# More key heads on VectorE and a 512-wide p V product in a decode attention kernel bound by its cache loads

## The chip, the cores and the metric

One core of one Trainium2 chip runs the whole program. The metric is the time of one execution on the device, in microseconds (us). Most executions of the kernel before agree within 0.3%, but it has a second cluster some 1 to 2 us higher in a few executions.

Five engines share the work: TensorE (PE, with its weight loads as PEld), VectorE (DVE), ScalarE (ACT), GpSimd (POOL) and SyncE (SP), which issues the loads. In the profile L286 is line 286 of the kernel.

## The reference, cut to what matters

```python
q = layernorm(x) @ wq                         # 32 heads of 128
k, v = k_cache[:, :, Sk-4096:], v_cache[:, :, Sk-4096:]
p = softmax(q k^T / sqrt(128))                # one query row per head, 4096 keys
s = (p v) @ wo                                # 512 outputs
out = x + s * silu(B(layernorm(x), w1, w2, w3, w4))
```

Each head reads 1 MB of keys and 1 MB of values in bf16, 64 MB in all; weights make it 79 MB. Nothing is used twice, so the loads are a floor under any schedule.

## The kernel before: the parts that matter

Heads come in groups of four. Every even head is scored on VectorE (a product with the broadcast query, then a sum along the head dimension), every odd one on TensorE: 32 transposes, evicted by ScalarE in four blocks of eight, then 32 matmuls of one column.

```python
if h % 2 == 0:
    nc.vector.tensor_tensor(out=prod, in0=kn, in1=q_bc[...], op=ALU.mult)
    nc.vector.tensor_reduce(out=s["sS"][:, hl // 2, :], in_=prod, axis=AX.X, op=ALU.add)
else:
    for b in range(NB):                       # NB = 4
        pt = ps_tr.tile([P, 8, P], BF16, tag="pt")          # three PSUM banks in turn
        for i in range(8):
            nc.tensor.transpose(pt[:, i, :], kn[:, b * 8 + i, :], ident_bf[:])
        nc.scalar.copy(out=kt[:, b * 8:(b + 1) * 8, :], in_=pt[:])
    ...
if hl == G - 1:
    softmax(g)        # two maxima, all-reduce on GpSimd, two subtractions, exp
```

Values follow four heads later. Each is 32 matmuls with one moving column (the probabilities) against 128x128 of values, summed in PSUM; the four heads of a group are scaled by one VectorE instruction. After a block of heads its outputs are repacked (`repack`) and multiplied with wo (`apply_wo`).

```python
for c in range(NC):                           # NC = 32
    nc.tensor.matmul(oT[:, k:k + 1], lhsT=v[:, c, :], rhs=s["pT"][..., c:c + 1],
                     start=(c == 0), stop=(c == NC - 1))
```

## Time and profile before

| | before |
|---|---|
| time, median of 3 | 198.69 us (198.66 to 200.05) |
| profiled span | 196.8 us |
| VectorE / TensorE / ScalarE busy | 126.9 / 119.4 / 69.3 us |
| mean granted TensorE clock | 0.667 |
| loads, from 30 to 187 us | about 424 GB/s, no gap |

How to read it: no engine is above 64% busy, and the chain that ended last is made of 71% loads. The lines are in the prediction. Two more are the busy share of the DMA engines in 40 slices (9 is 90% or more), and the granted clock in tenths.

```profile
PEclk9999999695585555576766667555555585575555
DMA  6999899999999999999999999999999999999960
```

The loads fill every slice to the end, and TensorE is at half clock for most of the second part.

### The profile page before, as it was taken

The numbers are of one execution on the slowest core, as the hardware profiler recorded it, in microseconds if no ns is written. First come the engines' busy times: TensorE is split into PE (matmuls) and PEld (weight loads), VectorE is DVE, ScalarE is ACT, GpSimd is POOL, SyncE is SP. The second block draws the span as 40 slices with busy tenths as digits, with TensorE's granted clock in tenths as the row PEclk, the third lists the DMA queues.
The fourth block names the chain that finished last, engine by engine and source line by source line (L and its number), as shares of the span: only waits on it lengthen the run. The fifth ranks groups of instructions, "written<-read, shape, count | busy, mean of one in ns | idle before, by whom it ended". The sixth has DMA issues, their size and how long they took to land.

```text
span 196.8 us, 5237 instructions
## 1 busy us (share of the span) xinstructions
PE 119.4 (61%) x2399; PEld 108.4 (55%) x2399; DVE 126.9 (64%) x140; ACT 69.3 (35%) x82; POOL 4.9 (3%) x17
## 2 busy tenths in 40 slices
PE   0315896851969474684829293756665654929443
PEld 0314745841969473583829292656565653929332
DVE  1225049998959993959387937959198929594301
ACT  2000329742565243070707070242525250707000
POOL 1011000000000000000000000000000000000000
PEclk9999999695585555576766667555555585575555
DMA  6999899999999999999999999999999999999960
GB/s 185 383 485 446 355 416 421 426 426 421 426 421 423 421 421 425 423 425 420 426 421 428 421 425 416 425 420 426 423 428 423 425 418 425 421 426 422 426 268 10
DMA packets 11349, 79.17 MB, mean 402 GB/s; under 512 B 1376, under 2 KB 1984, under 8 KB 2368
## 3 DMA queue, kind: packets, MB, share of 16 engines
q1 hardware_dynamic: 11176, 78.85, 96.3%
q8 instruction: 18, 0.29, 0.6%
q10 hardware_dynamic: 152, 0.00, 0.0%
q14 instruction: 3, 0.02, 0.0%
HBM read 78.84 MB, written 0.00 MB: 401 GB/s over the span
## 4 chain that ended last, share of the span: by engine, by line
DMA 71%; DVE 12%; issue 6%; PE 6%; ACT 2%; POOL 1%; SPq 0%; POOLq 0%
DMA kv<-in_A_v_cache_dram 40%; DMA kv<-in_A_k_cache_dram 30%; DVE sS L265 7%; DVE prod L262 3%; ACT kt L272 1%; PE a_ps L202 1%; PE qT_ps L221 1%; PE oT L364 1%; PE qb_ps L230 1%; PE h_ps L135 1%; PE y_ps L135 0%; PE ln_ps L140 0%; PE ln_ps L152 0%; ACT q_bc L232 0%; POOL ln_rstd_x L158 0%
## 5 line engine op out<-in xcount | busy, mean ns | idle before, releaser
L272 ACT COPY kt<-pt 128x1024 bf16<-128x1024 bf16 x64 | 60.2, 1025 | 73.0 <-PE pt L271 73.0
L265 DVE TENSOR_REDUCE sS<-prod 128x32 f32<-128x4096 bf16 x16 | 70.7, 4419 | 0.5
L271 PE MATMUL pt<-ident_bf,kv 128*128 128x128 bf16 x512 | 53.8, 298 | 18.2 <-DMA kv<-in_A_k_cache_dram 17.7
L271 PEld LDWEIGHTS <-kv 128*128 128x128 bf16 x512 | 49.8, 140 | 19.7 <-DMA kv<-in_A_k_cache_dram 18.7
L364 PEld LDWEIGHTS <-kv 128*128 128x128 bf16 x1024 | 30.0, 102 | 30.5 <-DMA kv<-in_A_v_cache_dram 22.8
L262 DVE TENSOR_TENSOR prod<-kv,q_bc 128x4096 bf16<-128x4096 bf16 x16 | 36.5, 2283 | 11.0 <-DMA kv<-in_A_k_cache_dram 8.8
L364 PE MATMUL oT<-pT,kv 128*128 128x1 bf16 x1024 | 32.6, 165 | 17.6 <-DMA kv<-in_A_v_cache_dram 17.3
L243 PE MATMUL sT<-qT_bf,kt 128*128 128x1 bf16 x512 | 20.4, 166 | 2.6 <-ACT kt L272 2.3
L243 PEld LDWEIGHTS <-kt 128*128 128x128 bf16 x512 | 18.3, 103 | 3.4 <-ACT kt L272 3.2
L300 PE MATMUL den_ps<-pT,ones_bf 128*128 128x128 bf16 x8 | 2.0, 253 | 16.9 <-ACT pT L294 16.9
L371 DVE TENSOR_TENSOR o<-oT,rden 128x4 bf16<-128x4 f32 x7 | 1.1, 162 | 17.3 <-PE oT L364 17.3
L294 ACT ACTIVATE pT<-e 128x128 bf16<-128x128 f32 x8 | 2.5, 309 | 16.5 <-DVE e L290 16.5
L140 PEld LDWEIGHTS ln_ps<-x_f,ones_f 128*128 128x128 f32 x4 | 1.0, 312 | 11.3 <-DVE x_f L182 6.4
L287 POOL PARTITION_ALL_REDUCE mb<-m x8 | 3.0, 373 | 162.5 <-DVE m L285 162.5
L205 ACT ACTIVATE a_bf<-a_ps 128x10 bf16<-128x10 f32 x1 | 0.2, 180 | 17.4 <-PE a_ps L202 17.4
L302 DVE TENSOR_REDUCE den<-den_ps 128x4 f32<-128x128 f32 x8 | 2.3, 292 | 5.5 <-PE den_ps L300 5.5
L135 PEld LDWEIGHTS <-ox 128*1 128x1 bf16 x112 | 2.5, 113 | 5.3 <-DVE ox L341 5.3
L367 DVE TENSOR_TENSOR o<-oT,rden 128x1 bf16<-128x1 f32 x4 | 0.6, 161 | 7.2 <-PE oT L364 7.2
L230 PE MATMUL qb_ps<-wq_sb,xn_rep 128*128 128x512 bf16 x16 | 5.2, 497 | 0.0
L135 PE MATMUL y_ps<-wo,ox 128*1 128x128 bf16 x112 | 3.7, 306 | 2.3 <-DVE ox L341 2.3
L140 PE MATMUL ln_ps<-x_f,ones_f 128*128 128x4 f32 x4 | 1.2, 365 | 5.9 <-DVE x_f L163 4.9
L290 DVE TENSOR_TENSOR e<-sS,mb 128x64 f32<-128x64 f32 x8 | 1.8, 224 | 3.9 <-POOL mb L287 3.9
(79 smaller groups left out, 48.2 us busy)
## 6 DMA issues: line engine op xcount, KB each, us to landing
kv<-in_A_k_cache_dram SPq DMA_DIRECT2D x32, 1024.0 KB, 19.7
kv<-in_A_v_cache_dram SPq DMA_DIRECT2D x32, 1024.0 KB, 19.7
wq_sb<-in_A_wq_dram SPq DMA_DIRECT2D x1, 4096.0 KB, 19.2
wo<-in_A_wo_dram SPq DMA_DIRECT2D x3, 1024.0 KB, 20.4
w_sb<-in_B_w_dram SPq DMA_DIRECT2D x1, 1376.0 KB, 7.9
w_sb<-in_B_w_dram SPq DMA_DIRECT2D x1, 1024.0 KB, 10.2
w_sb<-in_B_w_dram SPq DMA_DIRECT2D x1, 512.0 KB, 3.7
wo<-in_A_wo_dram SPq DMA_DIRECT2D x1, 512.0 KB, 19.8
```

Source lines behind the costliest of these rows:

```text
L135: nc.tensor.matmul(ps[32 * j:32 * j + 1, :], lhsT=col, rhs=w[0:k, j * P:(j + 1) * P], start=False, stop=last, skip_group_check=True)
L140: nc.tensor.matmul(ps[:], lhsT=ones_f[:], rhs=src_f, start=True, stop=True)
L230: nc.tensor.matmul(qb_ps[:], lhsT=xn_rep[:, c, :], rhs=wq_h[:, c, 2 * i:2 * i + 8:2, :], start=(c == 0), stop=(c == KC - 1))
L243: nc.tensor.matmul(sT[:, hl // 2, c:c + 1], lhsT=kt[:, c, :], rhs=qT_bf[:, h:h + 1], start=True, stop=True)
L262: nc.vector.tensor_tensor(out=prod[:], in0=kn[:], in1=q_bc[:, h // 2:h // 2 + 1, :].to_broadcast([P, NC, Dh]), op=ALU.mult)
L265: nc.vector.tensor_reduce(out=s["sS"][:, hl // 2, :], in_=prod[:], axis=AX.X, op=ALU.add)
L271: nc.tensor.transpose(pt[:, i, :], kn[:, b * 8 + i, :], ident_bf[:])
L272: nc.scalar.copy(out=kt[:, b * 8:(b + 1) * 8, :], in_=pt[:])
L287: nc.gpsimd.partition_all_reduce(mb[:], m1[:], channels=P, reduce_op=ReduceOp.max)
L294: nc.scalar.activation(out=pT[:], in_=e[:], func=ACT.Exp, scale=scale)
L302: nc.vector.tensor_reduce(out=den[:], in_=den_ps[:], axis=AX.X, op=ALU.add)
L364: nc.tensor.matmul(oT[:, k:k + 1], lhsT=v[:, c, :], rhs=s["pT"][:, hl % 2, hl // 2, c:c + 1], start=(c == 0), stop=(c == NC - 1))
```

## The change

The intent: use VectorE, which looks a third idle, for 20 heads instead of 16, so that TensorE and ScalarE have 12 heads to transpose instead of 16; and make the value product cheaper in instructions, eight matmuls with 512 moving columns of values instead of 32 with one. The eight matmuls leave, for each head, four rows of four blocks of 128 sums, of which only the block with the row's own number is wanted; four small fp32 matmuls with a selection matrix (`add`) pick and add these for a whole group. The last group keeps the narrow form. The PSUM bank of the new accumulator is taken from the transposes, which have two banks now, not three. Four tiny loads of x, which nothing reads, are issued behind the seventh key head (`i == 6`) among the loads.

```diff
-    ps_tr = ctx.enter_context(tc.tile_pool(name="ps_tr", bufs=3, space=PSUM))
+    ps_tr = ctx.enter_context(tc.tile_pool(name="ps_tr", bufs=2, space=PSUM))
+    ps_v = ctx.enter_context(tc.tile_pool(name="ps_v", bufs=1, space=PSUM))
     ... 
+    def places(g):                            # heads of a group: on VectorE, on TensorE
+        if g % 2 == 0:
+            return slice(0, 3, 1), slice(3, 4, 1)
+        return slice(0, 4, 2), slice(1, 4, 2)
     ... (queries, softmax and denominators in this order)
-        for c in range(NC):
-            nc.tensor.matmul(oT[:, k:k + 1], lhsT=v[:, c, :], rhs=s["pT"][:, hl % 2, hl // 2, c:c + 1], ...)
+            for c in range(0, NC, 4):
+                nc.tensor.matmul(s["ov"][32 * hl:32 * hl + 4], lhsT=s["pT"][:, hl, c:c + 4],
+                                 rhs=v[:, c:c + 4, :], start=False, stop=c == NC - 4, ...)
+            if hl == G - 1:
+                nc.scalar.copy(out=s["ov_sb"][:], in_=s["ov"][:])
     ...
+            def add(s=s, o=o, at=h - h0 - 3):
+                oT = ps_o.tile([P, G], FP32, tag="oT", name="oT")      # one buffer
+                for j in range(4):
+                    nc.tensor.matmul(oT[:], lhsT=s["ov_sb"][:, j, :], rhs=pick_f[:, j, :], ...)
+                nc.vector.tensor_tensor(out=o[:, at:at + G], in0=oT[:], in1=s["rden"][:], op=ALU.mult)
     ...
+        if i == 6:
+            for n in (1, 2, 4, 8):
+                mk = small.tile([n, D // n], BF16, name=f"mk{n}")
+                load(mk[:], A_x.rearrange("a b (p n) -> (a b p) n", p=n))
```

So even groups now have three heads on VectorE and one on TensorE, odd groups two and two.

More of the change, by code (lines that the diff above doesn't have):

```diff
@@ L214, with on_vector @@
     nc.scalar.activation(out=g_row[:], in_=bv[:], func=ACT.Silu)
-    qT_ps = ps_misc.tile([P, H], FP32, tag="misc", name="qT_ps")
-    for h in range(1, H, 2):
+    def places(g):
+        if g % 2 == 0:
+            return slice(0, 3, 1), slice(3, 4, 1)
+        return slice(0, 4, 2), slice(1, 4, 2)
+    def on_vector(h):
+        s_pl = places(h // G)[0]
+        return h % G in range(G)[s_pl]
+    pe_heads = [h for h in range(H) if not on_vector(h)]
+    ve_heads = [h for h in range(H) if h % 2 == 0] + list(range(1, H, 2 * G))
+    assert sorted(pe_heads + ve_heads) == list(range(H))
+    q_at = {h: i for i, h in enumerate(ve_heads)}
+    q_at.update({h: i for i, h in enumerate(pe_heads)})
+    qT_ps = ps_misc.tile([P, len(pe_heads)], FP32, tag="misc", name="qT_ps")
+    for i, h in enumerate(pe_heads):
         for c in range(KC):
-            nc.tensor.matmul(qT_ps[:, h:h + 1], lhsT=wq_sb[:, c, h * Dh:(h + 1) * Dh],
+            nc.tensor.matmul(qT_ps[:, i:i + 1], lhsT=wq_sb[:, c, h * Dh:(h + 1) * Dh],
                              rhs=xn_bf[:, c:c + 1], start=(c == 0), stop=(c == KC - 1))
-    qT_bf = small.tile([P, H], BF16, name="qT_bf")
-    nc.vector.tensor_copy(out=qT_bf[:, 1::2], in_=qT_ps[:, 1::2])
-    q_bc = small.tile([P, H // 2, Dh], BF16, name="q_bc")
+    qT_bf = small.tile([P, len(pe_heads)], BF16, name="qT_bf")
+    nc.vector.tensor_copy(out=qT_bf[:], in_=qT_ps[:])
+    q_bc = small.tile([P, len(ve_heads), Dh], BF16, name="q_bc")
     wq_h = wq_sb[:].rearrange("p c (h d) -> p c h d", d=Dh)
-    for i in range(0, H // 2, 4):
+    for i in range(0, len(ve_heads), 4):
         qb_ps = ps_tr.tile([P, 4, Dh], FP32, tag="pt", name="qb_ps")
+        h0, step = ve_heads[i], ve_heads[i + 1] - ve_heads[i]
         for c in range(KC):
-            nc.tensor.matmul(qb_ps[:], lhsT=xn_rep[:, c, :], rhs=wq_h[:, c, 2 * i:2 * i + 8:2, :],
+            nc.tensor.matmul(qb_ps[:], lhsT=xn_rep[:, c, :], rhs=wq_h[:, c, h0:h0 + 3 * step + 1:step, :],
                              start=(c == 0), stop=(c == KC - 1))
@@ L239, with qk @@
     rows_open(y_ps)
-    def qk(sT, hl, h, kt):
+    def qk(sT, i, h, kt):
         for c in range(NC):
-            nc.tensor.matmul(sT[:, hl // 2, c:c + 1], lhsT=kt[:, c, :], rhs=qT_bf[:, h:h + 1],
+            nc.tensor.matmul(sT[:, i, c:c + 1], lhsT=kt[:, c, :],
+                             rhs=qT_bf[:, q_at[h]:q_at[h] + 1],
                              start=True, stop=True)
+    pick_f = const.tile([P, 4, G], FP32, name="pick_f")
+    nc.vector.tensor_copy(out=pick_f[:], in_=ident_bf[:].rearrange("p (h i) -> p i h", h=G)[:, 0:4, :])
     pending = []
@@ L256, in k_head @@
                 "sT": ps_s.tile([P, G // 2, NC], FP32, tag="sT", name="sT"),
-                "sS": sm_pool.tile([P, G // 2, NC], FP32, tag="sS", name="sS"),
+                "sS": sm_pool.tile([P, G - 1, NC], FP32, tag="sS", name="sS"),
             }
         s = st[g]
-        if h % 2 == 0:
+        on_v, on_t = places(g)
+        if on_vector(h):
             prod = prod_pool.tile([P, NC, Dh], BF16, tag="prod", name="prod")
             nc.vector.tensor_tensor(out=prod[:], in0=kn[:],
-                                    in1=q_bc[:, h // 2:h // 2 + 1, :].to_broadcast([P, NC, Dh]),
+                                    in1=q_bc[:, q_at[h]:q_at[h] + 1, :].to_broadcast([P, NC, Dh]),
                                     op=ALU.mult)
-            nc.vector.tensor_reduce(out=s["sS"][:, hl // 2, :], in_=prod[:], axis=AX.X, op=ALU.add)
+            nc.vector.tensor_reduce(out=s["sS"][:, range(G)[on_v].index(hl), :], in_=prod[:], axis=AX.X, op=ALU.add)
         else:
@@ L274, in k_head @@
                     flush()
-            pending.append((s["sT"], hl, h, kt))
+            pending.append((s["sT"], range(G)[on_t].index(hl), h, kt))
             if hl == G - 1:
@@ L282, in softmax @@
         s = st[g]
-        m1 = sm_pool.tile([P, 2, G // 2], FP32, tag="m1", name="m1")
-        nc.vector.tensor_reduce(out=m1[:, 0, :], in_=s["sS"][:], axis=AX.X, op=ALU.max)
-        nc.vector.tensor_reduce(out=m1[:, 1, :], in_=s["sT"][:], axis=AX.X, op=ALU.max)
-        mb = sm_pool.tile([P, 2, G // 2], FP32, tag="mb", name="mb")
+        parts = []
+        for pl, src in zip(places(g), (s["sS"], s["sT"])):
+            n = len(range(G)[pl])
+            parts.append((pl, n, src[:, 0:n, :]))
+        m1 = sm_pool.tile([P, G], FP32, tag="m1", name="m1")
+        for pl, n, src in parts:
+            nc.vector.tensor_reduce(out=m1[:, pl], in_=src, axis=AX.X, op=ALU.max)
+        mb = sm_pool.tile([P, G], FP32, tag="mb", name="mb")
         nc.gpsimd.partition_all_reduce(mb[:], m1[:], channels=P, reduce_op=ReduceOp.max)
-        e = sm_pool.tile([P, 2, G // 2, NC], FP32, tag="e", name="e")
-        for i, src in enumerate((s["sS"], s["sT"])):
-            nc.vector.tensor_tensor(out=e[:, i], in0=src[:],
-                                    in1=mb[:, i, :].unsqueeze(2).to_broadcast([P, G // 2, NC]),
+        e = sm_pool.tile([P, G, NC], FP32, tag="e", name="e")
+        for pl, n, src in parts:
+            nc.vector.tensor_tensor(out=e[:, pl, :], in0=src,
+                                    in1=mb[:, pl].unsqueeze(2).to_broadcast([P, n, NC]),
                                     op=ALU.subtract)
-        pT = sm_pool.tile([P, 2, G // 2, NC], BF16, tag="pT", name="pT")
+        pT = sm_pool.tile([P, G, NC], BF16, tag="pT", name="pT")
         nc.scalar.activation(out=pT[:], in_=e[:], func=ACT.Exp, scale=scale)
@@ L357, in v_head @@
             softmax_den(g)
-            s["oT"] = ps_o.tile([P, G], FP32, tag="oT", name="oT")
+            if i == last_block:
+                s["oT"] = ps_o.tile([P, G], FP32, tag="oT", name="oT")
+            else:
+                s["ov"] = ps_v.tile([P, 4, Dh], FP32, tag="ov", name="ov")
+                nc.tensor.matmul(s["ov"][:], lhsT=zero_bf[:], rhs=v[:, 0:4, :], start=True, stop=False,
+                                 skip_group_check=True)
         if h == h0:
             o_blk[i] = sm_pool.tile([P, n], BF16, tag="o", name="o")
-        k = 2 * (hl % 2) + hl // 2
-        oT, o = s["oT"], o_blk[i]
-        for c in range(NC):
-            nc.tensor.matmul(oT[:, k:k + 1], lhsT=v[:, c, :], rhs=s["pT"][:, hl % 2, hl // 2, c:c + 1],
-                             start=(c == 0), stop=(c == NC - 1))
-        if i == last_block:
-            nc.vector.tensor_tensor(out=o[:, h - h0:h - h0 + 1], in0=oT[:, k:k + 1],
-                                    in1=s["rden"][:, k:k + 1], op=ALU.mult)
-        elif hl == G - 1:
-            nc.vector.tensor_tensor(
-                out=o[:, h - h0 - 3:h - h0 + 1].rearrange("p (a b) -> p b a", b=2),
-                in0=oT[:].rearrange("p (b a) -> p b a", b=2),
-                in1=s["rden"][:].rearrange("p (b a) -> p b a", b=2), op=ALU.mult)
+        o = o_blk[i]
+        if i == last_block:
+            oT = s["oT"]
+            for c in range(NC):
+                nc.tensor.matmul(oT[:, hl:hl + 1], lhsT=v[:, c, :], rhs=s["pT"][:, hl, c:c + 1],
+                                 start=(c == 0), stop=(c == NC - 1))
+            nc.vector.tensor_tensor(out=o[:, h - h0:h - h0 + 1], in0=oT[:, hl:hl + 1],
+                                    in1=s["rden"][:, hl:hl + 1], op=ALU.mult)
+        else:
+            for c in range(0, NC, 4):
+                nc.tensor.matmul(s["ov"][32 * hl:32 * hl + 4], lhsT=s["pT"][:, hl, c:c + 4],
+                                 rhs=v[:, c:c + 4, :], start=False, stop=c == NC - 4,
+                                 skip_group_check=True)
+            if hl == G - 1:
+                s["ov_sb"] = sm_pool.tile([P, 4, Dh], FP32, tag="ov_sb", bufs=2, name="ov_sb")
+                nc.scalar.copy(out=s["ov_sb"][:], in_=s["ov"][:])
         ready, later[:] = later[:], []
@@ L377, in v_head @@
             f()
-        if h == h0 + n - 1 and i < last_block:
+        if hl == G - 1 and i < last_block:
+            def add(s=s, o=o, at=h - h0 - 3):
+                oT = ps_o.tile([P, G], FP32, tag="oT", name="oT")
+                for j in range(4):
+                    nc.tensor.matmul(oT[:], lhsT=s["ov_sb"][:, j, :], rhs=pick_f[:, j, :],
+                                     start=(j == 0), stop=(j == 3))
+                nc.vector.tensor_tensor(out=o[:, at:at + G], in0=oT[:], in1=s["rden"][:], op=ALU.mult)
             def step(i=i, n=n):
@@ L381, in step @@
                 later.append(lambda: [apply_wo(i, t) for t in range(n)])
-            later.append(step)
+            later.append(lambda: [add(), later.append(step)] if h == h0 + n - 1 else add())
     v_pool = None
```

## The prediction

> **What bounds the kernel now.** I read the chain that ended last, then the group rows of the page, then VectorE in order of time, then the last microseconds. From the page: busy totals, chain by engine, and the rows of the two instructions of a head on VectorE and of the transpose eviction:
>
> ```profile
> PE 119.4 (61%) x2399; PEld 108.4 (55%) x2399; DVE 126.9 (64%) x140; ACT 69.3 (35%) x82; POOL 4.9 (3%) x17
> ...
> DMA 71%; DVE 12%; issue 6%; PE 6%; ACT 2%; POOL 1%; SPq 0%; POOLq 0%
> ...
> L265 DVE TENSOR_REDUCE sS<-prod 128x32 f32<-128x4096 bf16 x16 | 70.7, 4419 | 0.5
> L262 DVE TENSOR_TENSOR prod<-kv,q_bc 128x4096 bf16<-128x4096 bf16 x16 | 36.5, 2283 | 11.0 <-DMA kv<-in_A_k_cache_dram 8.8
> ```
>
> The transfers set the end: 71% of the chain is key and value loads, and from 30 us to 187 us the DMA engines move about 424 GB/s without a gap. VectorE's product waits 8.8 us for keys. But the share of 64% understates VectorE: its first head starts only at 27.4 us, when the queries are there, so 119.8 of the 158 us from 27 to 185 are busy, 76%. One cycle of it, from VectorE's timeline:
>
> ```profile
> 66.63 2.29 DVE L262 TENSOR_TENSOR prod<-kv,q_bc 128x4096 bf16<-128x4096 bf16 x1
> 68.95 4.42 DVE L265 TENSOR_REDUCE sS<-prod 128x32 f32<-128x4096 bf16 x1
> 73.41 0.22 DVE L284 TENSOR_REDUCE m<-sS 128x2 f32<-128x64 f32 x1
> 75.42 0.16 DVE L371 TENSOR_TENSOR o<-oT,rden 128x4 bf16<-128x4 f32 x1 [1.79 <-PE oT L364]
> 75.62 0.23 DVE L332 TENSOR_TENSOR spread<-o,mt 128x64 bf16<-128x64 bf16 x1
> 75.76 0.21 DVE L285 TENSOR_REDUCE m<-sT 128x2 f32<-128x64 f32 x1
> 76.47 0.23 DVE L290 TENSOR_TENSOR e<-sS,mb 128x64 f32<-128x64 f32 x1 [0.50 <-POOL mb L287]
> 76.61 0.22 DVE L290 TENSOR_TENSOR e<-sT,mb 128x64 f32<-128x64 f32 x1
> 77.52 0.29 DVE L302 TENSOR_REDUCE den<-den_ps 128x4 f32<-128x128 f32 x1 [0.69 <-PE den_ps L300]
> ...
> 78.38 0.27 DVE L341 TENSOR_REDUCE ox<-pick 128x8 bf16<-128x64 f32 x1
> 78.56 2.28 DVE L262 TENSOR_TENSOR prod<-kv,q_bc 128x4096 bf16<-128x4096 bf16 x1
> ```
>
> A head costs 73.41 - 66.63 = 6.78 us. The softmax is a round trip VectorE, GpSimd, VectorE, ScalarE, TensorE, VectorE, and VectorE waits in place (0.50 and 0.69 us), because the next product stands behind it. The end, from the timeline of all engines:
>
> ```profile
> 191.93 1.01 PE L364 MATMUL oT<-pT,kv 128*128 128x1 bf16 x32 [1.45 <-DMA kv<-in_A_v_cache_dram]
> 192.93 0.60 PE L135 MATMUL y_ps<-wo,o 128*1 128x128 bf16 x16
> 192.98 0.16 DVE L367 TENSOR_TENSOR o<-oT,rden 128x1 bf16<-128x1 f32 x1 [2.30 <-PE oT L364]
> 193.58 0.29 DVE L404 TENSOR_TENSOR y<-y_ps,g_row 128x128 f32<-128x128 f32 x1 [0.43 <-PE y_ps L135]
> ```
>
> The last value head's data starts its matmuls at 191.93; the block of heads 24 to 27 had been finished at 186.
>
> **What the Trainium skill says.** "TensorE: Matmul & The Clock Gate", Back-to-back issue gap: a moving operand of N columns costs N / 1.2 ns cold and N / 2.4 + 2.5 ns warm, thus 427 or 216 ns for 512. This trace agrees: the 16 qb_ps matmuls of 512 take 5.19 us, which is 8 at 0.43 and 8 at 0.216, and the clock record turns full in their middle. Part 1 there (clock gate) says a busy window of about 3.4 us must pass before the clock rises; the mean granted clock here is 0.667. "Runtime: NRT & Kernel Launch", Instruction fetch mechanics: instructions are refilled in 16 KiB blocks of 256. The queue table here agrees: 18 instruction packets, 0.29 MB. "DMA: Bandwidth & Descriptors", Why a DMA increments its semaphore by 16 and not by 1: a load of 1, 2, 4 or 8 rows uses only that many engines. No run here shows it yet.
>
> **The change part by part.**
> - VectorE takes 20 heads, not 16: four more at 6.78, +27.1 us. Even groups have three, odd groups two.
> - ScalarE loses 16 evictions of about 1 us and gains 7 of a 128x512 fp32 tile (0.59 us, the q_bc row). It had slack: no gain.
> - TensorE: 28 heads change from 32 one-column matmuls (1.0 us a head) to 8 of 512 columns: 8 x 0.216 = 1.73 us warm, 3.46 cold. Fewer instructions, but more time. Seven groups gain four fp32 matmuls; one fp32 128x4 matmul of the layer norm is two passes, 0.22 us apart and 0.37 long, so four take 7 x 0.22 + 0.37 = 1.9 us.
> - Startup: 4 more qb_ps, 16 fewer qT_ps matmuls: the first product starts 16 x 0.029 = 0.46 us earlier, and the release of the query weights moves about 1 us later, with key loads still in flight until 35 us. No effect.
> - Four tiny loads take four of the eight completion slots that the load queue uses in turn. For about 10 us four big loads are in flight instead of eight, still about 10 us of work. No effect either way.
> - Instructions: TensorE's listed ones fall from 4788 to 2929, so some 7 fewer fetch packets of 16 KB, at 424 GB/s about 0.3 us in the mean; perhaps 1.5 us on the engine that ends last. Counts only if transfers still set the end.
>
> **VectorE's schedule, laid out by hand** in the order of the built program, with e(g) the moment when group g's second subtraction ends:
> - Heads 0, 1, 2 start at 27.0 and end at 47.3; then the maximum, the product of head 4, and e(0) = 50.2. Heads 4 and 6 are through at 62. TensorE does values 0 to 2 (one cold, two warm: 7.0 us from 51), then key head 7 with value 3 (about 6): 64.4. So e(1) is about 65.5, where it was 58.8, and head 8, whose key landed at 55, starts about 12 us late.
> - Odd to even: 1.35 to the next product (softmax remainder), 3 x 6.78 = 20.3, and 1.3 for maxima, reduction and subtractions: 23.0.
> - Even to odd: VectorE alone needs 1.75 + 2 x 6.78 + 0.2 = 15.5. But the maximum of the TensorE heads waits for a chain in TensorE's program order that starts only with this softmax: denominators, repack and 32 output matmuls (76.83 to 79.72 before, 2.9) and the opening matmul (0.3), value a (1.7 to 3.5), keys with value b (5.1 to 8.3, paced by the four 0.94 us evictions), value c (1.7 to 3.5), keys with value d (5.4 to 8.3). Sum 17.1 warm, 27 cold; I take 19.5, the first value cold and the rest mostly warm. Plus 1.07 from the maximum to e: 20.6.
> - The pair is 43.6 us, while the loads bring eight heads in 42.35 (keys 14 and 30 landed at 87.6 and 172.3). So the delay of 12 us is never won back. e(7) = 65.5 + 23.0 + 3 x 20.6 + 2 x 23.0 = 196.3, against 183.7 before.
> - Then 0.7 to the denominators and four value heads of 1.0 us with 0.25 between, as at 185.90 and 187.16: last value product ends at 201.8, not 192.94: +8.9.
>
> Value buffers do not choke this: value 31 needs buffer 24 free at about 182 instead of 172, with 17 us of loads in flight.
>
> **Tail.** The single PSUM buffer of oT is held by the last group, and in the built order the addition of heads 24 to 27 now stands behind the last value matmul. So 0.25 (scaling), 1.9 (four fp32), then scaling to output matmuls 1.1 (0.20 + 0.25 + 0.21 + 0.21 + 0.23), 32 output matmuls 1.0, while before the end came 0.64 after the product: +3.6.
>
> Sum: 198.7 + 8.9 + 3.6 = 211.2.
>
> **Rivals.**
> 1. Transfers still set the end. For it: 64% on VectorE looks idle, and bytes are unchanged. Against: the wait-in-place above. Then only tail and fetches count: 198.7 + 3.6 - 0.3 to 1.5 = 201 to 202.
> 2. VectorE binds, but TensorE stays warm: chain 17.1, three pairs shorter by 2.4 each: 204. This is the side on which I may err most.
> 3. TensorE stays cold: chain 27, three times 7.5 more: 233. Against: the value matmuls stream densely, so they should lift the clock above 0.667.
> 4. A gain: fewer instructions and a higher clock pay off. That needs TensorE or ScalarE on the chain now; together they have 8% of it, and the tail grows anyway.
>
> **Range and chances.** Rival 1 gives the floor, 201; a half-cold TensorE gives 217. I keep my sum a little lower because VectorE's waits may overlap better than I laid out: 210.5, with 202.5 to 217. Slower by over 2% means over 202.7: 0.88. Within 2%: 0.1. Faster: 0.02.
>
> **What would show it.** VectorE near 154 us busy, hardly waiting for key loads after 60 us; the product after softmax 1 near 67 us; waits of 2 to 6 us on TensorE's sT before the maxima of the odd groups; the chain with VectorE and TensorE in front and the value loads nearly gone; DMA digits falling before the end; a granted clock above 0.7; fp32 oT matmuls after the last value product. If VectorE still waits for keys at 130 us and the last value product starts at its landing near 191, rival 1 holds and only the tail is left.

## The result, and the profile after

| same rounds, same chip | before | after |
|---|---|---|
| median of 4 | 199.37 us (198.66 to 200.19) | 211.28 us (209.07 to 211.63) |
| profiled span | 196.8 us | 209.3 us |
| VectorE / TensorE / ScalarE busy | 126.9 / 119.4 / 69.3 us | 153.3 / 129.3 / 59.5 us |
| mean granted clock | 0.667 | 0.821 |
| packets of instructions (q8) | 18 | 12 |

The kernel got slower: ratio 1.0573, 95% interval 1.0482 to 1.0663. A ratio here is the mean time of one kernel's runs over that of the other's of the same rounds, so it is not quite the ratio of the medians quoted.

The prediction counted by e(g), the moment when group g's second subtraction ends; the same mark is used here, read from VectorE's timeline, and a "stretch" is the time from one e to the next. First the page of the kernel after: busy totals, clock, DMA slices, chain by engine, and two group rows (busy, mean ns | idle before, releaser).

```profile
PE 129.3 (62%) x1522; PEld 78.1 (37%) x1522; DVE 153.3 (73%) x149; ACT 59.5 (28%) x74; POOL 6.9 (3%) x17
...
PEclk9999999755699996559999955589999755599955
DMA  6999999999999999999999999999999999996000
...
DVE 45%; PE 35%; issue 8%; ACT 7%; POOL 3%; POOLq 0%; ACTq 0%; DVEq 0%
...
L404 PE MATMUL ov<-kv,pT 128*4 128x512 bf16 x224 | 54.2, 428 | 1.2 <-DMA kv<-in_A_v_cache_dram 1.2
...
L313 DVE TENSOR_REDUCE m<-sT 128x1 f32<-128x32 f32 (+1 forms) x8 | 1.6, 203 | 15.9 <-PE sT L260 15.9
```

The loads are gone from the chain, where they had 71%, and the DMA digits fall three slices before the end: the data is there, the engines are late. VectorE waits 15.9 us for TensorE's scores in front of its maxima. VectorE in order of time, from one even softmax to the next odd one (duration in the second column, the wait and its releaser in brackets):

```profile
90.42 4.42 DVE L289 TENSOR_REDUCE sS<-prod 128x32 f32<-128x4096 bf16 x1
94.87 2.29 DVE L286 TENSOR_TENSOR prod<-kv,q_bc 128x4096 bf16<-128x4096 bf16 x1
97.20 4.42 DVE L289 TENSOR_REDUCE sS<-prod 128x32 f32<-128x4096 bf16 x1
101.65 0.22 DVE L313 TENSOR_REDUCE m<-sS 128x2 f32<-128x64 f32 x1
106.67 0.23 DVE L313 TENSOR_REDUCE m<-sT 128x2 f32<-128x64 f32 x1 [4.80 <-PE sT L260]
...
108.90 2.26 DVE L286 TENSOR_TENSOR prod<-kv,q_bc 128x4096 bf16<-128x4096 bf16 x1
```

VectorE is through with its two heads at 101.62, but the maximum of the TensorE heads comes only at 106.67. No product can start before that softmax is out of VectorE's way. What TensorE does meanwhile, from its own timeline:

```profile
86.77 0.26 PE L328 MATMUL den_ps<-pT,ones_bf 128*128 128x128 bf16 x1 [8.78 <-ACT pT L322]
...
89.73 3.58 PE L404 MATMUL ov<-kv,pT 128*4 128x512 bf16 x8
93.24 1.19 PE L295 MATMUL pt<-ident_bf,kv 128*128 128x128 bf16 x16
95.14 0.61 PE L295 MATMUL pt<-ident_bf,kv 128*128 128x128 bf16 x8 [0.71 <-ACT kt L296]
...
99.03 1.89 PE L404 MATMUL ov<-kv,pT 128*4 128x512 bf16 x8
100.86 1.07 PE L295 MATMUL pt<-ident_bf,kv 128*128 128x128 bf16 x16
...
104.26 1.89 PE L404 MATMUL ov<-kv,pT 128*4 128x512 bf16 x8
106.08 0.55 PE L260 MATMUL sT<-qT_bf,kt 128*128 128x1 bf16 x16
```

TensorE idled 8.78 us before the denominators. Then the four values and two key heads go through it one after the other: the first value cold (eight matmuls in 3.58 us), the later ones warm (1.89), each key pass about 5.8 us from its first transpose to the next value or to the last score (the second value stands inside the first pass, the fourth inside the second).

In the odd-to-even stretches three values stand directly behind one another, and there the trace shows what the text of the change does not: the matmuls of neighbouring heads, which write different rows of the accumulator, start in pairs (4 to 6 ns apart at 154 us), so that 24 of them take 3.62 to 4.10 us instead of 3 x 1.89. In the even-to-odd stretch a key pass stands between the values, and this is lost. A program that keeps the values together there was not tried. The end, from the timeline of all engines:

```profile
201.65 0.16 DVE L400 TENSOR_TENSOR o<-oT,rden 128x1 bf16<-128x1 f32 x1 [1.08 <-PE oT L398]
201.86 1.87 PE L417 MATMUL oT<-pick_f,ov_sb 128*128 128x4 f32 x8 [0.26 <-DVE o L400]
...
204.84 0.60 PE L136 MATMUL y_ps<-wo,ox 128*1 128x128 bf16 x16 [0.48 <-DVE ox L369]
205.22 0.64 PE L136 MATMUL y_ps<-wo,o 128*1 128x128 bf16 x16
205.92 0.29 DVE L451 TENSOR_TENSOR y<-y_ps,g_row 128x128 f32<-128x128 f32 x1 [1.13 <-PE y_ps L136]
```

The scaling of the last value product ends at 201.65 + 0.16 = 201.81 (before, by the prediction's third fence: 192.98 + 0.16 = 193.14); the fp32 addition of heads 24 to 27 and their repacking follow in the open, and the final product starts at 205.92, 4.11 us behind that scaling, where it was 0.44.

### The profile page after: what moved, and what is told of

The parts are those of the page before. It is cut to its first block, busy times and chain, and to the rows that moved or that the text cites. A ratio compares the mean times of both kernels' runs of the same rounds, so it can differ in the third digit from the quotient of the medians.

```text
span 209.3 us, 3495 instructions
## 1 busy us (share of the span) xinstructions
PE 129.3 (62%) x1522; PEld 78.1 (37%) x1522; DVE 153.3 (73%) x149; ACT 59.5 (28%) x74; POOL 6.9 (3%) x17
## 4 chain that ended last, share of the span: by engine, by line
DVE 45%; PE 35%; issue 8%; ACT 7%; POOL 3%; POOLq 0%; ACTq 0%; DVEq 0%
DVE sS L289 25%; PE ov L404 17%; DVE prod L286 13%; ACT kt L296 5%; PE pt L295 5%; PE sT L260 3%; POOL mb L315 2%; PE y_ps L136 2%; PE oT L398 2%; DVE e L318 1%; PE a_ps L203 1%; ACT pT L322 1%; DVE m L313 1%; PE den_ps L328 1%; PE oT L417 1%
## 5 line engine op out<-in xcount | busy, mean ns | idle before, releaser
L289 DVE TENSOR_REDUCE sS<-prod 128x32 f32<-128x4096 bf16 x20 | 88.4, 4419 | 0.6
L296 ACT COPY kt<-pt 128x1024 bf16<-128x1024 bf16 x48 | 45.6, 1022 | 64.9 <-PE pt L295 64.8
L404 PE MATMUL ov<-kv,pT 128*4 128x512 bf16 x224 | 54.2, 428 | 1.2 <-DMA kv<-in_A_v_cache_dram 1.2
L286 DVE TENSOR_TENSOR prod<-kv,q_bc 128x4096 bf16<-128x4096 bf16 x20 | 45.7, 2284 | 2.6 <-ACT q_bc L249 2.2
L295 PE MATMUL pt<-ident_bf,kv 128*128 128x128 bf16 x384 | 29.6, 229 | 14.8 <-ACT kt L296 8.6
L295 PEld LDWEIGHTS <-kv 128*128 128x128 bf16 x384 | 24.5, 103 | 25.0 <-issue 17.6
L404 PEld LDWEIGHTS <-pT 128*4 128x4 bf16 x224 | 16.4, 91 | 33.6 <-issue 17.5
L260 PE MATMUL sT<-qT_bf,kt 128*128 128x1 bf16 x384 | 14.8, 164 | 1.3 <-ACT kt L296 1.3
L313 DVE TENSOR_REDUCE m<-sT 128x1 f32<-128x32 f32 (+1 forms) x8 | 1.6, 203 | 15.9 <-PE sT L260 15.9
L417 PE MATMUL oT<-pick_f,ov_sb 128*128 128x4 f32 x56 | 8.2, 270 | 1.4 <-ACT ov_sb L409 1.1
L417 PEld LDWEIGHTS oT<-pick_f,ov_sb 128*128 128x128 f32 x56 | 7.6, 210 | 2.0 <-ACT ov_sb L409 1.7
## 6 DMA issues: line engine op xcount, KB each, us to landing
wo<-in_A_wo_dram SPq DMA_DIRECT2D x3, 1024.0 KB, 20.6
```

The source lines that it names most:

```text
L260: nc.tensor.matmul(sT[:, i, c:c + 1], lhsT=kt[:, c, :], rhs=qT_bf[:, q_at[h]:q_at[h] + 1], start=True, stop=True)
L286: nc.vector.tensor_tensor(out=prod[:], in0=kn[:], in1=q_bc[:, q_at[h]:q_at[h] + 1, :].to_broadcast([P, NC, Dh]), op=ALU.mult)
L289: nc.vector.tensor_reduce(out=s["sS"][:, range(G)[on_v].index(hl), :], in_=prod[:], axis=AX.X, op=ALU.add)
L404: nc.tensor.matmul(s["ov"][32 * hl:32 * hl + 4], lhsT=s["pT"][:, hl, c:c + 4], rhs=v[:, c:c + 4, :], start=False, stop=c == NC - 4, skip_g ...
L417: nc.tensor.matmul(oT[:], lhsT=s["ov_sb"][:, j, :], rhs=pick_f[:, j, :], start=(j == 0), stop=(j == 3))
```

## The experiments

All twelve give the right result. Each was timed against the kernel before on the same chip in the same rounds; that kernel's median was 198.70 us in the first four runs, 198.73 in the next four, 198.77 in the next three and 198.77 in the last one. "Base" says from which kernel an edit starts. Ratios are to the kernel before of the same rounds; where two variants are compared with each other, as in "below the kernel after", it is by their medians and traces, from different rounds.

### One half of the change at a time

**Heads alone** (base after): 20 and 12 heads, two transpose banks and tiny loads stay, all values in the narrow form (the edit is cut to its main lines).

```diff
+    def wide(g):
+        return False
-            if i == last_block:               # the narrow form
+            if i == last_block or not wide(g):
```

> 20 and 12 heads as in the changed kernel, but every group's values in the old form of 32 one-column matmuls. My theory (20 heads on VectorE fit as long as TensorE's chain behind the even softmax stays under VectorE's 15.5 us): the pair of groups falls under the 42.35 us of the loads, the delay of about 7 us at the start is won back, 198 to 200.5 us. Rival (VectorE's 27 us of extra work are the loss by themselves): 205 us or more.

Measured: 200.08 us (199.95 to 202.21), ratio 1.0074 (1.0018 to 1.0131), as expected. VectorE is 153.1 us busy, as in the kernel after, but does not pay: the stretch from an even softmax to the next odd one takes 17.1 and 17.4 us in the middle, from odd to even 23.0, so 40.0 and 40.4 for a pair of groups. The last value head waits for its data again:

```profile
193.04 1.01 PE L401 MATMUL oT<-pT,kv 128*128 128x1 bf16 x32 [1.27 <-DMA kv<-in_A_v_cache_dram]
```

**Values alone** (base after): 16 and 16 heads again, values 512 wide.

```diff
-        if g % 2 == 0:
-            return slice(0, 3, 1), slice(3, 4, 1)
-    ve_heads = [h for h in range(H) if h % 2 == 0] + list(range(1, H, 2 * G))
+    ve_heads = [h for h in range(H) if h % 2 == 0]
```

> Values in the 512-wide form as in the changed kernel, but heads split 16 and 16 as before. My theory: transfers set the last value's landing again, and only the tail is paid: 198.7 + 3.6 - up to 1.5 for fewer instruction fetches = 200.8 to 202.3. Rival (the slower value product alone delays TensorE's chain): 205 us or more. If both this and the run with the heads alone come out near the kernel before, the loss needs both parts.

Measured: 203.42 us (203.32 to 203.58), ratio 1.0215 (1.0162 to 1.0268), so 1.1 above the expectation. From its list of VectorE's waits (total, times, longest):

```profile
DVE m L311 <- PE sT L258: 26.4, 7, 5.3
```

VectorE waits for TensorE in all seven stretches, 26.4 us, more than in the kernel after, and yet this is not what sets the end: where no load is waited for a stretch is 18.6 to 20.6 us, e(7) comes at 186.3, and the last value again waits for its load (its matmuls start at 193.05). It starts 1.1 us later than before (191.93), which fits the slower packets of the section on the tiny loads, and behind it stands the fp32 tail, 4.1 us from the end of the last value's scaling to the final product.

So each half stays under the 42.35 us in which eight heads are loaded. With heads alone VectorE needs 23.0 us in one stretch of a pair, but the other is 17.1 to 17.4. With values alone TensorE needs up to 20.6 in each, which is 41.2 for two. With both, the one stretch is VectorE's (22.6) and the other TensorE's (21.5 to 21.9), and the pair is 44.0 to 44.6.

### Where the values hurt

**Even groups narrow** (base after; odd groups stay wide):

```diff
+    def wide(g):
+        return g % 2 == 1
```

> The changed kernel, but the value heads of even groups (three key heads on VectorE, one on TensorE) go back to 32 one-column matmuls with VectorE's scaling of four columns; odd groups keep the 512-wide form. My theory: the loss sits in the stretch from an even softmax to the next odd one, where the value heads of the even group and two key heads pass through TensorE one after the other before the maximum of the TensorE heads. With narrow values there that chain falls under VectorE's own 15.5 us, a pair of groups takes about 40.5 us, less than the 42.35 in which eight heads are loaded, the last value head waits for its data again, and heads 24 to 27 leave no fp32 addition behind it: 199.5 to 201.5 us, e(7) near 187. Rival: it is TensorE's total load of 512-wide matmuls, wherever they stand: removing half of it gives about half of the loss back, 204 to 206, and the same in the run with the odd groups narrow.

Measured: 201.99 us (201.40 to 202.12), ratio 1.0142 (1.0099 to 1.0185): 9.3 us of the loss gone, and 0.5 above the range expected. Stretches from even to odd are 18.6, 19.0 and 21.9 us, from odd to even 22.6, 21.6 and 21.6. e(7) comes at 188.65 us, 7.9 earlier than in the kernel after; the other 1.3 are behind it, where the edit also removes the fp32 addition of heads 24 to 27. Loads are in the chain again, though the last four value heads, against the expectation, wait for none:

```profile
DMA 50%; DVE 22%; PE 12%; issue 9%; POOL 2%; ACT 2%; POOLq 0%; ACTq 0%; SPq 0%; DVEq 0%
```

Part of what is left has a name: the odd group's fp32 addition needs the one output buffer that the next group's narrow values hold, so it comes late and VectorE waits 1.96 us for it in front of a maximum, three times.

**Odd groups narrow** (base after; even groups stay wide):

```diff
+    def wide(g):
+        return g % 2 == 0
```

> The mirror image: odd groups narrow, even groups 512-wide. My theory: the stretch behind the even softmax keeps its 512-wide values (waits of 4 to 6 us on sT before the maxima of odd groups stay) and the fp32 addition of heads 24 to 27 still stands behind the last value head: 210 to 211.5 us, as the changed kernel. Rival (TensorE's total load): 204 to 206. A third way: the narrow values let TensorE's clock sink, so that the 512-wide ones cost 3.5 instead of 1.8 us each: 213 or more.

Measured: 217.11 us (216.57 to 217.53), ratio 1.0900 (1.0846 to 1.0955). A miss of the theory's time by 6 us. The third way's time would fit, but not its mechanism: in the three stretches the first value takes 3.57, 2.90 and 3.57 us and the last two are warm (1.89), as in the kernel after. The even-to-odd stretches are what the theory said, 21.8, 20.7 and 21.6 us, with waits on the scores of 4.0 to 5.1 us. But the odd-to-even ones grew from 22.6 to 25.0, 25.1 and 25.1:

```profile
85.33 1.87 PE L423 MATMUL oT<-pick_f,ov_sb 128*128 128x4 f32 x8 [8.69 <-DVE o L407]
...
87.24 0.16 DVE L425 TENSOR_TENSOR o<-oT,rden 128x4 bf16<-128x4 f32 x1 [1.96 <-PE oT L423]
```

The addition of the even group waits 8.7 us until the odd group's outputs have left the single buffer, and then VectorE, which has the scaling in front of the maximum of the even group, stands for 1.96 us. It is the mechanism of the tail, now once per pair: 7.3 us in the three odd-to-even stretches, more than e(7) lost (202.84 for 196.54), as the other stretches gave 1.0 back. TensorE's total load as such (the rival) is refuted by the two runs together: the same kind of halving gave minus 9.3 in one and plus 5.8 in the other, and also in the second the even-to-odd stretches stayed about as long as in the kernel after.

### The third bank

**Three banks for the transposes** (base after; taken from the scores):

```diff
-    ps_tr = ctx.enter_context(tc.tile_pool(name="ps_tr", bufs=2, space=PSUM))
+    ps_tr = ctx.enter_context(tc.tile_pool(name="ps_tr", bufs=3, space=PSUM))
-    ps_s = ctx.enter_context(tc.tile_pool(name="ps_s", bufs=2, space=PSUM))
+    ps_s = ctx.enter_context(tc.tile_pool(name="ps_s", bufs=1, space=PSUM))
```

> The changed kernel with three PSUM banks for the transposes again, as before the change; the bank is taken from the scores of the TensorE heads (one buffer instead of two). Theory: the third bank matters only in the stretch behind an even softmax, where the third quarter of the second key head's transposes waits 0.7 us for ScalarE's first eviction and the fourth eviction comes 0.8 late. So the three even-to-odd stretches get about 0.8 shorter each (21.6 to 20.8), e(7) falls from 196.5 to 194.0 to 195.5, the time to 208.5 to 210.3. Rival 1: two banks are what makes TensorE's chain long at all: 3 us or more per stretch, 201 to 203. Rival 2: nothing, 210.5 to 211.6; or the single buffer of the scores makes a wait of its own, above 211.6.

Measured: 206.85 us (205.58 to 207.68), ratio 1.0388 (1.0347 to 1.0428), 4.4 us below the kernel after, where 1 to 2.8 were expected: the third bank was worth more than the waits of 0.7 and 0.8 us from which it was worked out. From TensorE's timeline of this run:

```profile
92.33 1.51 PE L295 MATMUL pt<-ident_bf,kv 128*128 128x128 bf16 x24
94.11 0.61 PE L295 MATMUL pt<-ident_bf,kv 128*128 128x128 bf16 x8 [0.26 <-ACT kt L296]
...
97.33 1.89 PE L404 MATMUL ov<-kv,pT 128*4 128x512 bf16 x8
```

Three blocks of transposes now go through at once, and the first key pass of the stretch takes 97.33 - 92.33 = 5.00 us, where the kernel after has 99.03 - 93.24 = 5.79. The even-to-odd stretches are 20.2, 19.6 and 20.3 us (after: 21.5, 21.9, 21.5), and e(7) is 190.8 instead of 196.5. So the bank that the new accumulator took is a part of the loss of its own; it is not all of it.

### The tail

**All additions in another pool** (base after):

```diff
             def add(...):
-                oT = ps_o.tile([P, G], FP32, tag="oT", name="oT")
+                oT = ps_misc.tile([P, G], FP32, tag="misc", name="oT")
```

> The changed kernel with one edit: the fp32 addition of a group goes into the ps_misc bank, so that the addition of heads 24 to 27 no longer waits for the last group's oT bank. My theory (3.6 us of the loss is this tail, the rest is a delay before it): 211.3 - 3.6 = 207.7 us, and the last value product is followed by 0.4 to 0.6 us to the start of the final product, not 4.1. Rival (the tail is hidden or moves elsewhere, because the same 32 output matmuls and the repack only shift): 210 to 211.

Measured: 216.39 us (216.19 to 216.66), ratio 1.0869 (1.0821 to 1.0918). A miss of 9 us. The tail did shrink (0.38 us from the last scaling to the final product), but that pool also has one buffer, which the denominators and the repacking use in turn, so every addition went right behind a softmax's denominators. In the even-to-odd stretch that is TensorE's critical chain (from its timeline of all engines):

```profile
87.96 1.87 PE L417 MATMUL oT<-pick_f,ov_sb 128*128 128x4 f32 x8 [0.38 <-DVE den L330]
...
91.17 1.02 PE L136 MATMUL y_ps<-wo,ox 128*1 128x128 bf16 x32 [0.62 <-DVE ox L369]
```

The output matmuls started 3.86 us after the denominators' (87.31), where it was 88.24 - 86.77 = 1.47 in the kernel after. The even-to-odd stretches became 22.8, 24.2 and 22.7 us instead of 21.5, 21.9 and 21.5, the others stayed at 22.6, and e(7) went from 196.5 to 201.9. By accident this run shows again that this stretch sets the time: work put there lengthens every pair.

**Only the addition of heads 24 to 27 moved** (base after):

```diff
+                if g == H // G - 2:
+                    oT = ps_misc.tile([P, G], FP32, tag="misc", name="oT")
+                else:
+                    oT = ps_o.tile([P, G], FP32, tag="oT", name="oT")
```

> The changed kernel, but the fp32 addition of heads 24 to 27 alone writes to a tile of the other pool, so that it need not wait for the last group's output tile and stands before the last value heads. Theory (the tail costs 3.6 us in the open): the end moves 3.6 forward, less what the addition and the repacking put before the last four value heads on TensorE (1.9 of fp32 matmuls and up to 1 of others): 208.0 to 210.0, e(7) unchanged at 196.5, final product under 1 us after the last output matmul of the last head. Rival (the tail is hidden or paid for elsewhere, as in the run with all groups moved): 211 or more.

Measured: 209.53 us (208.94 to 210.21), ratio 1.0528 (1.0481 to 1.0575). The medians say 1.75 less than the kernel after, the profiled spans 0.9 less (208.4 for 209.3), and the intervals of the two ratios overlap. From the timeline:

```profile
197.35 1.05 PE L420 MATMUL oT<-pick_f,ov_sb 128*128 128x4 f32 x8 [0.38 <-DVE den L330]
...
200.38 0.60 PE L136 MATMUL y_ps<-wo,ox 128*1 128x128 bf16 x16 [0.48 <-DVE ox L369]
...
205.00 0.29 DVE L454 TENSOR_TENSOR y<-y_ps,g_row 128x128 f32<-128x128 f32 x1 [0.39 <-PE y_ps L136]
```

The tail behind the last value's scaling is 0.39 us instead of 4.11, but that scaling ends at 204.61 instead of 201.81: the addition now stands before all four last value heads, the repacking before three of them. Only 0.9 of 3.7 us is won. Here the last softmax sets the end and the work runs one piece after the other, so it hardly matters on which side of the last values that work lies; it would matter if the last load set the end (not tried).

### The tiny loads

**Without them** (base after): the block `if i == 6: ...` is dropped.

> The changed kernel without the four tiny loads. My theory: no effect, 211.3 within 0.7 us. Rival (they cost, since for some 10 us only four large loads are in flight and the eight completion slots are shifted): faster by 1 us or more. Second rival (they help): slower by 1 us or more.

Measured: 210.06 us (208.93 to 210.64), ratio 1.0544 (1.0500 to 1.0587). The median lies 1.2 below the kernel after, outside the 0.7 expected and at the rival's number; but it is from other rounds, the intervals of the ratios overlap, the profiled spans differ by 0.4 us (208.9 for 209.3), and e(7) comes at 196.3 for 196.5. No effect that these runs could show.

In the trace of the kernel before the median 8 KB packet takes 309 ns, in those of the kernel after and of all variants up to here 312 or 313. That can hardly show in a kernel whose loads do not set the end, so the kernel before itself was given the loads.

**The kernel before with the four loads** (base before): the same block of four lines added.

> The kernel before with the four tiny loads of x added and nothing else. The prediction said: no effect either way, so within 0.3 us of the kernel before. Rival, from the traces: in all traces with these loads an 8 KB packet of keys or values takes 313 ns and not 309, and the last value head starts 1.1 us later although fewer instruction packets are fetched; if these loads are the cause, the kernel gets 1.0 to 1.6 us longer, which this one, bound by its loads, must show in full.

Measured: 200.78 us (200.54 to 200.89), ratio 1.0086 (1.0052 to 1.0120). The prediction's "no effect either way" does not hold here.

**One load of 16 rows** (base before):

```diff
+        if i == 6:
+            mk = small.tile([16, D // 16], BF16, name="mk16")
+            load(mk[:], A_x.rearrange("a b (p n) -> (a b p) n", p=16))
```

> The kernel before with one tiny load of 16 rows instead of four with 1, 2, 4 and 8 rows. Theory A (the uneven number of rows, 15, leaves the engines in another order or phase for the rest of the stream): 16 rows give every engine the same, so 198.5 to 199.2 us and 8 KB packets at 309 ns. Theory B (any tiny load in the stream, or the pause it makes in issuing, brings the slower mode): 200.3 to 200.9 us, packets at 312 ns, as with the four.

Measured: 200.69 us (200.41 to 201.72), ratio 1.0082 (1.0060 to 1.0104): the time of theory B of that text, not A; the next run shows that B's cause was wrong too.

**Its tile without the load** (base before):

```diff
+        if i == 6:
+            mk = small.tile([16, D // 16], BF16, name="mk16")
+            nc.gpsimd.memset(mk[:], 0.0)
```

> The kernel before with the tile of the 16-row load, but not the load: the tile is cleared once by GpSimd at the start and never read. All buffers that are allocated after it lie at the same places as in the run with the 16-row load; the transfers are those of the kernel before. Theory A (the small transfer, or the pause it makes in issuing, brings the slower mode of the stream): 198.5 to 199.2 us, 8 KB packets at 309 ns. Theory B (the tile shifts the buffers in on-chip memory, and that makes each 8 KB packet 3 to 4 ns longer; this would also explain the slower packets of the changed kernel without tiny loads): 200.4 to 200.9 us, packets at 312 ns.

Measured: 200.64 us (200.45 to 201.72), ratio 1.0093 (1.0049 to 1.0137). The load is gone and the 1.9 us are still there. The last value head of this run, to be held against 191.93 in the prediction's third fence:

```profile
193.81 1.01 PE L364 MATMUL oT<-pT,kv 128*128 128x1 bf16 x32 [1.64 <-DMA kv<-in_A_v_cache_dram]
```

So it is not the transfers but the places of the buffers (this is theory B of the text above). In the built program of the kernel before all value buffers start at a multiple of 256 bytes in each partition (the first at 154,624 = 604 x 256) and key buffers 64 bytes past one. The packets, from the traces, between 65 and 180 us without the few above 340 ns:

| kernel | key / value buffers past a multiple of 256 B | share of 8 KB packets at exactly 309 ns | usual mean of a 10 us window |
|---|---|---|---|
| before | 64 / 0 | 78% | 309.8 ns |
| before, tile of 16 rows, no load | 128 / 64 | 21% | 313.2 ns |
| before, one load of 16 rows | 128 / 64 | 19% | 313.3 ns |
| before, four tiny loads | 192 / 128 | 22% | 313.3 ns |
| after | 224 / 32 | 12% | 314.2 ns |

In the kernel before, stretches of packets at exactly 309.0 ns alternate with stretches around 310.4, as the loads of values and keys alternate. 3.4 ns more in 309.8 is 1.1%; over the 160 us of the stream an estimate of 1.8 us, and 1.9 was measured. That the shift of the buffers causes it is shown (the last run changes nothing else but a clearing of 64 bytes in each of 16 partitions; it moves every buffer allocated behind it by 64 bytes, not the load buffers alone); that the multiple of 256 bytes is the criterion is only the pattern of this table. The missing run is one with a pad that puts all buffers at multiples of 256. It also stays open why a few of the 11 executions of the kernel before in each series lie 1 to 2 us higher, as at 200.82 us with a span of 198.8, with its buffers where they always are.

### A candidate

**16 and 16 heads, wide values for groups 0 to 5, narrow ones after, no tiny loads** (base after; the rest of the edit is that of the runs above):

```diff
+    def wide(g):
+        return g < 6
```

> A candidate to beat the kernel before: 16 heads on each engine as before, 512-wide values for groups 0 to 5 only, the last two groups in the old narrow form (so that no fp32 addition stands behind the last value head), and no tiny loads. Theory: the stages stay under the loads' 42.35 us per pair, the tail is that of the kernel before, and some 4 fewer instruction packets of 16 KB leave the DMA engines a little more time: 197.8 to 199.0 us, the kernel before or up to 0.5 % better. Rival: without the tiny loads the stream still falls into the slower of its two modes (8 KB packets at 312 ns instead of 309), as in the changed kernel without tiny loads: 199.8 to 200.8.

Measured: 200.44 us (199.93 to 201.21), ratio 1.0076 (1.0049 to 1.0103). No gain, and the number of the rival: its buffers lie 96 and 160 bytes past a multiple of 256 and the packets take 313 ns. But the last four value heads wait for no load; the end is set by e(7) at 188.2, in whose stretch (24.0 us) VectorE waits 2.0 us for the addition of group 5, which had to wait for the output buffer. 14 instruction packets instead of 18 do not make up for that. No version tried beats the kernel before.

## Why the prediction was right

It said 210.5 us (its sum: 211.2), and 211.28 was measured. The sum is right, though some of its terms are not:

- **What bounds the kernel**: as said. The loads left the chain, VectorE and TensorE have 45% and 35% of it, and the first half of the argument, that a VectorE at 64% has no third to give, is confirmed by its waits.
- **VectorE's 27.1 us**: 153.3 - 126.9 = 26.4 us more busy time, as worked out, but taken alone worth nothing that can be seen (heads alone: 200.08 us, less than the kernel before with its buffers shifted). They count only through the stretch odd to even, 22.6 us measured for 23.0.
- **Even to odd, 20.6 us**: 21.5, 21.9 and 21.5 measured. This is the term that was undersized. The first value was cold and the others warm, as taken. The key passes took 5.8 us each, where the warm sum had 5.1 and 5.4. That is the third transpose bank, which the prediction does not mention; with it the first key pass takes 5.00 us and the stretches fall to 20.2, 19.6 and 20.3.
- **e(1) = 65.5**: 63.8 measured; the first three values took 6.09 us where 7.0 were laid out, since the matmuls of neighbouring heads overlap, which the prediction did not count. The errors cancel: -1.7 here, +3.1 in three even-to-odd stretches and -1.2 in three odd-to-even ones leave e(7) = 196.5 for 196.3. That the total comes out so close is in part luck.
- **Last value product +8.9**: by the end of its scaling, 201.81 - 193.14 = +8.7.
- **Tail +3.6**: 4.11 - 0.44 = +3.7, with the fp32 matmuls of 1.87 us where they were put. But "the tail costs 3.6" must not be read as "without it 3.6 are saved": moved, it gave 0.9 in the profile.
- **Tiny loads, no effect**: right for the transfers (the run with the load and the run with its tile alone agree within 0.1 us) and right for the changed kernel; wrong for the reason that their tiles shift the buffers, which costs 1.9 us wherever the loads set the end.
- **Rivals.** Rival 1, transfers still bound, 201 to 202, is right for each half tried alone in its mechanism, as the last value waits for its load in both, but not in its number: heads alone, which have no fp32 tail, took 200.08, and with values alone it was 203.42, as the tail comes on top of the slower packets, a term that rival 1 lacked. Rival 2, TensorE warm, 204: the first value of each stretch was cold in the middle of the run, so it did not come; even with three banks it is 206.85. Rival 3 and rival 4 are far off.
- **What would show it**: waits of 4.8 to 5.3 us on the scores in the odd groups of the steady part (2 to 6 said), the product after softmax 1 at 64.86 (67 said), the clock 0.821, the DMA digits falling early, the fp32 matmuls behind the last value: all seen.
- **Small slips.** The instruction packets fell by six (18 to 12), not seven, and the page's own counts for TensorE are 2 x 2399 before and 2 x 1522 after, not 4788 and 2929. Rival 3's 233 adds its 22.5 us to 210.5, while rival 2's 204 is taken from 211.2. No range hangs on either.

On the skill's words in the prediction: that a load of 1, 2, 4 or 8 rows uses only that many engines now has support. The four tiny loads add 30 packets to the kernel before (11,379 for 11,349): 15 rows and 15 writes of 4 bytes, one for each engine if each writes its completion once. The load of 16 rows adds 32.

## What to carry to other kernels

An engine with a third of its time free has not got it to give, if it stands in line with another engine at every softmax: lay out each stretch between two synchronisations with each engine's own time, take the larger one, and compare the sum with the loads. A PSUM bank or a shared single buffer is part of that time, since it decides at which place of its program an engine stands and waits. And before a change of 1% is judged in a kernel bound by loads, look whether the new tiles have moved the load buffers.

## What the Trainium skill lacked or had wrong

- "DMA: Bandwidth & Descriptors", How a descriptor splits into AXI transactions, says that reads start at 256-byte boundaries and that a descriptor off such a boundary costs extra beats. It says nothing of the destination in SBUF. Here the sources stay where they are, and moving the SBUF buffers by a 64-byte tile made the kernel 1.9 us (0.9%) slower, with 8 KB packets at 313.2 ns instead of 309.8 in the mean.
- "SBUF — State Buffer", Operand start alignment, treats alignment, in its own words, as "legality, not speed", and says that its runs timed nothing; the same 1.9 us belong there as a cost.
- "Runtime: NRT & Kernel Launch", Instruction fetch mechanics, calls the cost of crossing a block "mostly hidden". In the trace of the kernel before, beside a 16 KB instruction packet one 8 KB packet takes 773 to 856 ns instead of 309, in all 18 cases. What it costs in the end was not isolated: 14 packets instead of 18 brought nothing that could be seen.
- "TensorE: Matmul & The Clock Gate", Back-to-back issue gap, agrees for one head alone: the starts of its wide matmuls lie 216 ns apart warm and 427 cold (eight take 1.89 and 3.58 us with the end of the last). It also gives about 131 ns for a sustained stream with 512 columns; here only the streams of several heads, which overlap, come towards it, at best 24 matmuls in 3.62 us, 151 ns each.
- No page has a number for what one PSUM buffer costs that two uses must take in turn. Here that cost 2.4 us per pair of groups (odd groups narrow) and 5.3 us up to the last softmax (all additions in one pool).
